# Rope attention and two MLPs on one core: when the next pair's q and k are prepared beside the attention units

## The chip, the cores and the metric

The kernel runs on one core of a Trainium2 chip. The core has five instruction streams that matter here: TensorE (PE; PEld are its weight loads), VectorE (DVE), ScalarE (ACT), GpSimd (POOL) and SyncE (SP), which issues the DMAs. The metric is the device time of one execution in microseconds (us), lower is better; of several executions the median is taken.

## The reference, cut to what matters

Attention over 4 batches and 8 heads of 576 tokens and 64 dimensions, and behind it two MLPs over the 2304 tokens (512 to 2048 to 512), each with an activation of its own.

```python
def rotate(x):
    x1, x2 = (x[..., :half], x[..., half:])
    return np.concatenate([x1 * cos - x2 * sin, x1 * sin + x2 * cos], axis=-1)
q_rot, k_rot = (rotate(q), rotate(k))
scores = scale * np.matmul(q_rot, k_rot.transpose(0, 1, 3, 2))
scores = scores - np.max(scores, axis=-1, keepdims=True)
attn = np.exp(scores)
attn = attn / (np.sum(attn, axis=-1, keepdims=True) + 1e-09)
return np.matmul(attn, v).astype(np.float32)
...
h = x @ w_in
g = np.where(pos, h, np.where(neg, 0.0, (h + beta) ** 2 / (4.0 * beta)))
return (g @ w_out).astype(np.float32)
```

The second MLP is the same with `s * relu(h) ** 2 + b` in between.

## The kernel before

Precision comes from parts: an fp32 operand is split into a high part (rounded to the format that TensorE reads at full rate) and a low part (the rest), and products are summed over the parts.

**Attention.** Two heads of a batch make a pair; there are 16 pairs (0 to 15), and each has nine units (`UNITS`): four blocks of 128 query rows for either head, and a fifth in the middle (unit 4 of the pair) that holds the 64 remaining rows of both heads. The units of all pairs are counted through, 0 to 143; unit 36 is the first of pair 4. A unit goes through all engines: TensorE makes its scores (`sc`, L357, in one of two PSUM buffers), VectorE takes the row maxima (`nm`, L359), ScalarE the exponentials (`p`, L364), TensorE transposes `p` (`tp`, L379), and VectorE or ScalarE copies that out of PSUM (`pt`, L386 for the second head, L384 for the first, L382 for the unit in the middle). After each half of a pair the products with v follow (`av`, `rm`), and a result `u`.

**Preparing a pair.** Each pair's q and k must be rotated and split before its first score:

- q: GpSimd multiplies it by the table (four instructions, `qin<-qin,tab_sb`), VectorE adds the two halves (L294, "the sum"), ScalarE writes the high part (L308, once for each head) and VectorE the low part (L309, once for each head), into one of two tiles `qs0`, `qs1`, which the pairs use in turn.
- k: GpSimd multiplies (four instructions, `kin<-kin,tab_sb`) and adds (two), ScalarE casts the high part (L321, "the cast"), GpSimd subtracts (two more, `fp32r` in the rows), and SP copies the parts on to `kh` (four DMAs, L326) and `kz` (two, L329), of which there are two tiles each as well.

**Beside it.** ScalarE, VectorE and GpSimd also convert the MLP's weights, half a slice at a time (`convert()`: L134 first on ScalarE, L135 to L138 on VectorE, L139 on ScalarE, two steps on GpSimd), and from pair 6 on TensorE works through the first MLP's products (L181, `h` and `y`) between the units. After the attention the rest of the MLPs follows, with an order on TensorE that is written out by hand.

**What sets the order.** Before that, a scheduler puts the instructions of each engine in an order when the program is built, from the order in which the code names them and what each needs; on the chip each engine then works through its own list in order. `with tc.issue_after(x):` asks that what is recorded inside, as far as it runs on x's engine, stands behind x in that list. It makes no wait on the chip by itself. `maxs[n]` and `exps[n]` are the maxima and the exponentials of unit n, `parts[1]` the cast and the subtraction of pair 1's k. `do_load(n)`, called once for each unit, names the preparations. Before, it named q's whole preparation of pair i+1 at unit 0 of pair i, and k's at unit 2, tied to nothing (but pair 2's q); so the scheduler places each step as early as its inputs and its buffers let it.

Of the kernel before, what the change touches and what calls it, by code (L numbers as in the profile page):

```python
# [14 lines left out]
ALU = mybir.AluOpType  # L15
# [51 lines left out]
def kernel(ctx, tc, qq, kk, vv, tab, ww1, ww2, s, b, out):  # L67
    nc = tc.nc
# [516 lines left out]
    def do_load(n):  # L585
        if n == 0:
            with tc.issue_after(turned):
                turned_by(tq, QP[1])
                lay_q(0, tq, QP[1], None)
        elif n in (1, 2):  # L590
            with tc.issue_after(maxs[n]):
                if n == 1:
                    turned_by(tq, QP[2])
                else:
                    lay_q(0, tq, QP[2], None)
        if n < len(units):
            i, k = units[n]
            if i + 1 < NPAIR:
                if i == 0 and k in (2, 6):
                    with tc.issue_after(maxs[k]):  # L600
                        turned_by(qk_in["q", 1], HALVES[k // 6])
                if i == 0 and k in (4, 5, 7, 8):
                    with tc.issue_after(maxs[k]), tc.issue_after(exps[k - 1]):
                        lay_q(1, qk_in["q", 1], HALVES[k // 6], None, [int(k in (5, 8))])
                if i and k == 0:
                    with ExitStack() if i > 1 else tc.issue_after(parts[1][1]), ExitStack() if i > 1 else tc.issue_after(maxs[9]):
                        rope_pair(i + 1, "q", nc.gpsimd, nc.vector, None)
                elif k == 2:
                    with ExitStack() if i else tc.issue_after(exps[2]), ExitStack() if i else tc.issue_after(lowest):
                        rope_pair(i + 1, "k", nc.gpsimd, nc.gpsimd, [nc.gpsimd, nc.vector])  # L610
                elif k == 7:
                    load_v(i + 1)
                elif k in (4, 6) and i + 2 < NPAIR:
                    load_qk(i + 2, "q" if k == 4 else "k")

        if n in range(33, 51, 2) or n in range(70, 110, 4):
            with tc.issue_after(exps[n - 14]):
                convert()

        if n in PARK_AT and parking:  # L620
            with tc.issue_after(exps[n - 4]):
                parking.pop(0).park(wst, scratch)()
# [581 lines left out]
```

## Time and profile before

| | |
|---|---|
| median of 3 runs | 1116.61 us (1113.03 to 1118.2) |
| profiled execution | 1117.65 us, of which the profile's span is 1115.9 us |
| busy share of the span | PE 96%, PEld 88%, DVE 69%, ACT 57%, POOL 38% |
| units of attention | 144, exponentials from 15.3 to 417.9 us |
| granted TensorE clock | 0.998 on the mean |

The span runs from the first to the last instruction. A busy time is the time that an engine's instructions cover; TensorE's ends are modelled, so small gaps between its instructions do not show. In the rows, "x14" is a count, and a row of the timeline that ends in [0.70 <-DVE pt L386] says that the engine was idle for 0.70 us before this instruction and that line 386 on VectorE ended it.

### The profile page before, as it was taken

The page shows a single profiled execution, that of the slowest core. Times are in us where ns is not written, and L with a number is a line of the kernel's source. Part 1 is how long each engine was busy: PE and PEld are TensorE (multiplying, and loading weights), DVE is VectorE, ACT ScalarE, POOL GpSimd, SP SyncE. Part 2 cuts the span into 40 slices and gives each one's busy share as a digit, 9 for nine tenths or more (in the row PEclk, how much of TensorE's full clock was granted, in tenths as well). Part 3 has the DMA queues.
Part 4 walks back from the last instruction along what each step waited for, and adds up shares of the span by engine and source line. Part 5 has one row for each costly group of instructions (what it writes and reads, how often), then busy time and mean ns, then how long its engine had stood idle before and what let it go on. Part 6 is the DMA issues. An engine that isn't in the chain of part 4 may idle for free.

```text
span 1115.9 us, 20052 instructions
## 1 busy us (share of the span) xinstructions
PE 1074.3 (96%) x7296; PEld 981.3 (88%) x7296; DVE 775.0 (69%) x1445; ACT 631.0 (57%) x1440; POOL 426.9 (38%) x564
## 2 busy tenths in 40 slices
PE   5899999989999999999999999999999999999998
PEld 3666788878888889999999999999999999999997
DVE  7888987768576663454757667866777778677754
ACT  5777776766666665454545455474554448334431
POOL 6998977686473332332544445110212110000000
PEclk9999999999999999999999999999999999999999
DMA  8665856656675544655465673231322853221221
GB/s 240 168 191 167 253 160 208 207 165 188 202 227 166 174 151 138 220 171 190 149 183 203 211 238 116 86 112 59 113 89 90 301 171 116 82 83 42 80 63 36
DMA packets 109762, 173.24 MB, mean 155 GB/s; under 512 B 29408, under 2 KB 80608, under 8 KB 109664
## 3 DMA queue, kind: packets, MB, share of 16 engines
q1 hardware_dynamic: 109664, 171.97, 49.1%
q8 instruction: 57, 0.93, 0.4%
q14 instruction: 41, 0.34, 0.1%
HBM read 110.10 MB, written 48.56 MB: 142 GB/s over the span
## 4 chain that ended last, share of the span: by engine, by line
PE 81%; DVE 5%; DMA 5%; POOL 3%; ACT 3%; issue 2%; SPq 0%; POOLq 0%; ACTq 0%
PE hps L181 15%; PE sum L940 14%; PE yps L856 6%; PE yps L855 6%; PE yps L854 6%; PE y L181 5%; PE sc L357 5%; PE yps L790 4%; PE yps L791 4%; PE yps L792 4%; PE av L405 4%; PE h L181 4%; PE tp L379 3%; DMA wraw<-in_ww 1%; DMA kz<-kin 1%
## 5 line engine op out<-in xcount | busy, mean ns | idle before, releaser
L181 PE MATMUL hps<-xh,w 128*128 128x288 f32 (+4 forms) x640 | 163.4, 324 | 0.0
L357 PE MATMUL sc<-kh,qs 128*128 128x288 f32 x336 | 102.7, 328 | 24.5 <-ACT p L364 13.5
L359 DVE TENSOR_REDUCE nm<-sc 128x1 f32<-128x576 f32 x144 | 106.5, 748 | 24.9 <-PE sc L357 24.4
L364 ACT ACTIVATE p<-sc,nm 128x576 f32<-128x576 f32 x144 | 106.7, 742 | 28.6 <-DVE nm L359 26.2
L948 ACT ACTIVATE four<-four,b_sb,s_sb 128x480 f32<-128x480 f32 x64 | 47.4, 782 | 127.2 <-DVE four L947 127.2
L856 PE MATMUL yps<-gh,w 128*128 128x480 f32 (+1 forms) x320 | 118.5, 370 | 0.0
L854 PE MATMUL yps<-gh,w 128*128 128x480 f32 (+1 forms) x320 | 118.4, 370 | 0.0
L855 PE MATMUL yps<-gl,w 128*128 128x480 f32 (+1 forms) x320 | 118.4, 370 | 0.0
L96 POOL TENSOR_TENSOR wm<-wm,w 128x256 f32<-128x256 f32 x80 | 69.5, 888 | 119.1 <-ACT w L139 62.5
L181 PEld LDWEIGHTS hps<-xh,w 128*128 128x128 f32 x640 | 113.2, 188 | 1.0
L357 PEld LDWEIGHTS sc<-kh,qs 128*128 128x128 f32 x336 | 63.5, 192 | 45.7 <-ACT p L364 27.0
L181 PE MATMUL hps<-xl,w 128*128 128x288 f32 (+4 forms) x320 | 103.7, 324 | 0.0
L790 PE MATMUL yps<-gh,w 128*128 128x288 f32 (+3 forms) x288 | 93.2, 324 | 1.4 <-DVE yp L797 0.7
L357 PE MATMUL sc<-kz,qs 128*128 128x288 f32 x336 | 93.8, 301 | 0.0
L791 PE MATMUL yps<-gl,w 128*128 128x288 f32 (+3 forms) x288 | 92.8, 322 | 0.0
L792 PE MATMUL yps<-gh,w 128*128 128x288 f32 (+3 forms) x288 | 92.8, 322 | 0.0
L379 PE MATMUL tp<-ident,p 128*128 128x128 f32 x576 | 87.2, 276 | 4.0 <-DVE pt L386 3.4
L96 POOL TENSOR_TENSOR wm<-wm,raw 128x256 f32<-128x256 f32 x16 | 12.6, 806 | 176.8 <-ACT raw L139 176.8
L181 PE MATMUL y<-gh,w 128*128 128x288 f32 x320 | 75.0, 305 | 2.0 <-DVE ptr L397 0.9
L379 PEld LDWEIGHTS tp<-ident,p 128*128 128x128 f32 x576 | 70.5, 142 | 6.2 <-DVE pt L386 4.1
L405 PE MATMUL av<-pt,vin 128*64 128x256 f32 (+1 forms) x512 | 75.7, 417 | 0.0
L107 DVE TENSOR_TENSOR gl<-hps,gh 128x288 fp32r<-128x288 f32 (+4 forms) x88 | 46.4, 527 | 40.4 <-ACT gh L103 40.2
(154 smaller groups left out, 2905.9 us busy)
## 6 DMA issues: line engine op xcount, KB each, us to landing
wraw<-in_ww SPq DMA_DIRECT2D x56, 512.0 KB, 4.4
w<-parkd SPq DMA_DIRECT2D x24, 512.0 KB, 6.1
kin<-in_k SPq DMA_DIRECT2D x15, 576.0 KB, 4.4
qin<-in_q SPq DMA_DIRECT2D x15, 576.0 KB, 4.8
kh<-kin SPq DMA_DIRECT2D x60, 144.0 KB, 2.9
parkd<-wraw SPq DMA_DIRECT2D x16, 512.0 KB, 3.2
xs<-y1d SPq DMA_DIRECT2D x32, 240.0 KB, 2.7
xd<-u SPq DMA_DIRECT2D x16, 288.0 KB, 2.7
```

The lines of the kernel that those rows point to most:

```text
L181: m = nc.tensor.matmul(out_ps, l, r, start=(i == 0), stop=(i == n - 1))
L357: nc.tensor.matmul(sc[:, half, o:o + n], l, r[:, k0:k0 + n], start=m == 0, stop=m == len(todo) - 1)
L364: exps[i * 9 + k] = nc.scalar.activation(p, sc[:, :, :288], AF.Exp, bias=nm, scale=1.0, accum_out=sums_t[i][:, col:col + 1]).ins
L379: m = nc.tensor.transpose(v[:, c, :], p[:, c * P:(c + 1) * P], ident)
L405: nc.tensor.matmul(ps[j * D:(j + 1) * D, :n], v[:, kt, j, :], pt[g][:, kt, j, :], start=kt == 0, stop=False)
L790: nc.tensor.matmul(acc, wh, gh, start=f == 0, stop=False)
L791: nc.tensor.matmul(acc, wh, gl, start=False, stop=False)
L792: nc.tensor.matmul(acc, wl, gh, start=False, stop=last)
L854: nc.tensor.matmul(acc, wh, gh, start=f == 0, stop=False)
L855: nc.tensor.matmul(acc, wh, gl, start=False, stop=False)
L856: nc.tensor.matmul(acc, wl, gh, start=False, stop=last)
L940: nc.tensor.matmul(acc, l, r, start=j == 0, stop=j == len(t) - 1)
```

## The change

The preparation of pair i+1 is taken apart for i of 1 and more (pairs 2 to 15) and named at different units of pair i: q's product at unit 0; q's sum at unit 4, behind the maxima of unit 3; the two heads' parts at units 5 and 6, behind the maxima of the unit before and the exponentials of the one before that; k's product and sum at unit 2, as before; k's cast, subtraction and copies at unit 3, the cast behind the exponentials of unit 2. Apart from that, `convert()` at units 70 to 106 has its first step on ScalarE behind the exponentials of ten units back, where it was fourteen. No instruction is added or removed; instructions stand elsewhere in the engines' lists.

```diff
                 if i == 0 and k in (4, 5, 7, 8):
                     with tc.issue_after(maxs[k]), tc.issue_after(exps[k - 1]):
                         lay_q(1, qk_in["q", 1], HALVES[k // 6], None, [int(k in (5, 8))])
+                if i:
+                    t = qk_in["q", i + 1]
+                    if k == 0:
+                        with ExitStack() if i > 1 else tc.issue_after(parts[1][1]):
+                            pool_tt(out=t, in0=t, in1=tab_sb, op=ALU.mult)
+                    elif k == 4:
+                        with tc.issue_after(maxs[n - 1]):
+                            nc.vector.tensor_tensor(out=t[:, 1], in0=t[:, 0], in1=t[:, 1], op=ALU.add)
+                    elif k in (5, 6):
+                        with tc.issue_after(maxs[n - 1]), tc.issue_after(exps[n - 2]):
+                            lay_q(i + 1, t, WHOLE[0], None, [k - 5])
                 if i and k == 0:
-                    with ExitStack() if i > 1 else tc.issue_after(parts[1][1]), ExitStack() if i > 1 else tc.issue_after(maxs[9]):
-                        rope_pair(i + 1, "q", nc.gpsimd, nc.vector, None)
+                    pass
                 elif k == 2:
                     with ExitStack() if i else tc.issue_after(exps[2]), ExitStack() if i else tc.issue_after(lowest):
-                        rope_pair(i + 1, "k", nc.gpsimd, nc.gpsimd, [nc.gpsimd, nc.vector])
+                        if i == 0:
+                            rope_pair(i + 1, "k", nc.gpsimd, nc.gpsimd, [nc.gpsimd, nc.vector])
+                        else:
+                            t = qk_in["k", i + 1]
+                            pool_tt(out=t, in0=t, in1=tab_sb, op=ALU.mult)
+                            pool_tt(out=t[:, 1], in0=t[:, 0], in1=t[:, 1], op=ALU.add)
+                elif k == 3 and i:
+                    with tc.issue_after(exps[n - 1]):
+                        lay_k(i + 1, qk_in["k", i + 1], WHOLE[0], None)
                 elif k == 7:
                     load_v(i + 1)
...
         if n in range(33, 51, 2) or n in range(70, 110, 4):
-            with tc.issue_after(exps[n - 14]):
+            with tc.issue_after(exps[n - (10 if n > 60 else 14)]):
                 convert()
```

What it does to the lists is shown at three places. VectorE before, at units 39 to 41 (in pair 4): the maxima (L359) of units 39 and 40, and behind them the sum for `qin_1595`, the q of pair 7.

```order
L359 TENSOR_REDUCE nm_1225<-sc_1220 128x1
L386 COPY pt_1209<-tp_1243 128x4x128
L359 TENSOR_REDUCE nm_1264<-sc_1253 128x1
L294 TENSOR_TENSOR qin_1595<-qin_1595 128x576
L359 TENSOR_REDUCE nm_1284<-sc_1279 128x1
L386 COPY pt_1209<-tp_1302 128x4x128
L420 RECIPROCAL sume_1340<-sume_1340 128x5
```

VectorE after, at units 39 to 41; the sum (now L612) is that of `qin_966`, the q of pair 5, and its two low parts follow.

```order
L359 TENSOR_REDUCE nm_1210<-sc_1205 128x1
L612 TENSOR_TENSOR qin_966<-qin_966 128x576
L386 COPY pt_1194<-tp_1238 128x4x128
L359 TENSOR_REDUCE nm_1259<-sc_1248 128x1
L309 SCALAR_TENSOR_TENSOR qs1_108<-qin_966,qs1_108 64x576
L359 TENSOR_REDUCE nm_1280<-sc_1275 128x1
L386 COPY pt_1194<-tp_1300 128x4x128
L309 SCALAR_TENSOR_TENSOR qs1_108<-qin_966,qs1_108 64x576
L420 RECIPROCAL sume_1340<-sume_1340 128x5
```

The sum stood three pairs ahead of its use and stands one pair ahead now; sum and parts are in one place, each between the maxima of two units, and in ten of the fourteen pairs the sum stands directly in front of a copy of `pt` (in four before).

ScalarE before, at units 19 and 20 (in pair 2), with the cast of `kin_775`, the k of pair 4.

```order
L134 ACTIVATE wa_1019<-wraw_1017 128x512
L438 COPY r_656<-rm_651 128x384
L321 CAST kin_775<-kin_775 128x576
L384 COPY pt_686<-tp_688 128x4x128
L364 ACTIVATE p_668,sums_595<-sc_661,nm_666 128x576
```

ScalarE after, from the exponentials of unit 29 to those of unit 31 (in pair 3): the same cast, and the high parts of `qin_727`, the q of pair 4.

```order
L364 ACTIVATE p_902,sums_834<-sc_895,nm_900 128x576
L321 CAST kin_775<-kin_775 128x576
L364 ACTIVATE p_902,sums_834<-sc_921,nm_926 128x576
L308 ACTIVATE qs0_107<-qin_727 64x576
L384 COPY pt_910<-tp_968 128x4x128
L364 ACTIVATE p_962,sums_834<-sc_949,nm_960 128x576
L308 ACTIVATE qs0_107<-qin_727 64x576
```

The cast moved ten units back here, and 3 to 18 units over the pairs; the high parts moved by 3 to 7 units.

GpSimd before, around the subtraction of pair 4's k (the last row with `kin_775`): its two sums, the factors `eb` of a result, and the product of pair 5's q stand ahead of it.

```order
L96 TENSOR_TENSOR kin_775<-kin_775 128x288
L96 TENSOR_TENSOR kin_536<-kin_536 128x288 x2
L96 TENSOR_TENSOR kin_775<-kin_775 128x288
L422 COPY eb_643<-sume_640 128x256
L96 TENSOR_TENSOR qin_970<-qin_970,tab_sb_106 128x2x144 x4
L96 TENSOR_TENSOR kin_775<-kin_775 128x288 x2
```

GpSimd after, around the same subtraction: the products of pair 5's q and k and the steps of a conversion (`wm`, `w`) stand ahead of it.

```order
L96 TENSOR_TENSOR qin_966<-qin_966,tab_sb_106 128x2x144 x4
L96 TENSOR_TENSOR wm_1084<-wm_1084,w_1080 128x256 x2
L96 TENSOR_TENSOR kin_1014<-kin_1014,tab_sb_106 128x2x144 x4
L422 COPY eb_877<-sume_874 128x256
L96 TENSOR_TENSOR w_1080<-wm_1084,wa_1083 128x256 x2
L96 TENSOR_TENSOR kin_775<-kin_775 128x288 x2
L96 TENSOR_TENSOR kin_1014<-kin_1014 128x288 x2
```

The subtraction moved back behind work for pair 5. The first steps of the seven conversions in the second batch (L134 on ScalarE) stood behind the exponentials of units 68, 72, 78, 80, 84, 88 and 91, and stand behind those of 69, 73, 77, 80, 83, 85 and 90 now. Behind the attention all lists are the same.

## Rows read from the trace of the kernel before

**Rows 1.** The page, part 1: busy time, share of the span, instructions.
```profile
PE 1074.3 (96%) x7296; PEld 981.3 (88%) x7296; DVE 775.0 (69%) x1445; ACT 631.0 (57%) x1440; POOL 426.9 (38%) x564
```
**Rows 2.** Busy time by stretch: us, PE, PEld, DVE, ACT, POOL (instructions), clock, DMA share, GB/s.
```profile
33.00:134.00 101.00, 93.07 (x678) 66.61 (x677) 87.44 (x142) 77.33 (x183) 90.65 (x118) 1.00 0.68 197
134.00:300.00 166.00, 153.15 (x1160) 132.83 (x1159) 124.57 (x223) 114.72 (x285) 119.00 (x160) 0.99 0.61 186
300.00:418.00 118.00, 116.67 (x913) 104.30 (x913) 79.86 (x150) 80.58 (x201) 47.70 (x70) 1.00 0.61 185
```
**Rows 3.** TensorE's waits from 33 to 418 us: total, times, longest.
```profile
PE sc L357 <- ACT p L364: 10.4, 13, 1.9
PE tp L379 <- DVE pt L386: 3.4, 3, 1.7
```
**Rows 4.** VectorE's waits from 33 to 418 us.
```profile
DVE qin L294 <- POOL qin L96: 12.3, 7, 3.5
...
DVE qs L309 <- ACT qs L308: 3.5, 6, 0.8
```
**Rows 5.** ScalarE's waits from 33 to 418 us.
```profile
ACT kin L321 <- POOL kin L96: 3.3, 4, 1.2
...
ACT qs L308 <- PE sc L357: 2.4, 5, 1.0
```
**Rows 6.** Timeline from 33.8 to 42 us: start, length, engine, line, tiles, idle time before.
```profile
33.86 1.33 DVE L294 TENSOR_TENSOR qin<-qin 128x576 f32<-128x576 f32 x1
...
36.57 0.66 PE L379 MATMUL tp<-ident,p 128*128 128x128 f32 x4 [1.03 <-DVE pt L386]
...
40.54 0.74 ACT L364 ACTIVATE p<-sc,nm 128x576 f32<-128x576 f32 x1 [1.82 <-DVE nm L359]
...
41.42 0.40 PE L357 MATMUL sc<-kh,qs 128*128 128x288 f32 x1 [1.69 <-ACT p L364]
```
**Rows 7.** Timeline from 101.3 to 105 us.
```profile
101.51 1.27 DVE L294 TENSOR_TENSOR qin<-qin 128x576 f32<-128x576 f32 x1 [1.88 <-POOL qin L96]
...
104.09 0.44 PE L392 MATMUL tr<-ident,p 128*128 128x128 f32 x2 [0.70 <-DVE pt L386]
```
**Rows 8.** Timeline of TensorE at six of its stalls.
```profile
51.59 0.40 PE L357 MATMUL sc<-kh,qs 128*128 128x288 f32 x1 [0.27 <-ACT p L364]
...
72.81 0.40 PE L357 MATMUL sc<-kh,qs 128*128 128x288 f32 x1 [1.23 <-ACT p L364]
...
109.86 0.40 PE L357 MATMUL sc<-kh,qs 128*128 128x288 f32 x1 [1.19 <-ACT p L364]
...
125.93 0.40 PE L357 MATMUL sc<-kh,qs 128*128 128x288 f32 x1 [0.62 <-ACT p L364]
...
195.78 0.66 PE L379 MATMUL tp<-ident,p 128*128 128x128 f32 x4 [0.69 <-DVE pt L386]
...
362.90 0.40 PE L181 MATMUL y<-gh,w 128*128 128x288 f32 x1 [0.21 <-ACT pt L382]
```
**Rows 9.** The sum's line: count, shortest, median and longest (ns), first and last start.
```profile
L294 DVE TENSOR_TENSOR qin<-qin x14: 879/1266/1345, 33.9 to 315.6; 128x576 f32<-128x576 f32 x14
```
**Rows 10.** Timeline: k's cast and subtraction, unit 29's exponentials, pair 4's first score.
```profile
57.02 0.68 ACT L321 CAST kin<-kin 128x576 fp32r<-128x576 f32 x1
...
62.45 2.51 POOL L96 TENSOR_TENSOR kin<-kin 128x288 fp32r<-128x288 f32 x2
...
75.01 1.75 POOL L96 TENSOR_TENSOR kin<-kin 128x288 fp32r<-128x288 f32 x2 [0.78 <-ACT kin L321]
...
78.00 0.74 ACT L364 ACTIVATE p<-sc,nm 128x576 f32<-128x576 f32 x1 [0.43 <-DVE nm L359]
...
89.04 0.40 PE L357 MATMUL sc<-kh,qs 128*128 128x288 f32 x1
```
**Rows 11.** The copies on to `kz` (L329): from issue to landing.
```profile
DMA to landing us min/median/max: 2.4/3.6/5.2
```
**Rows 12.** Busy time from 152 to 157 us, columns as in rows 2.
```profile
152.00:157.00 5.00, 4.26 (x21) 4.25 (x22) 3.40 (x7) 4.64 (x12) 5.00 (x7) 0.66 0.45 134
```

## Prediction, before the result was known

> **What bounds the kernel now.** I read the page first: TensorE is busy for 1074.3 of 1115.9 us [rows 1]. The change removes none of its work, so what can be won or lost is its idle time of 41.6 us, and of that only what lies where the lists differ, from unit 9 to the last (33 to 418 us). The stretches [rows 2] say how much that is: 7.9 us in 33 to 134 (attention alone), 12.9 in 134 to 300 and 1.3 in 300 to 418 (with the MLP in between), 22.1 in all. In the first stretch VectorE and GpSimd are busy for 87 and 90% as well: there a step that stands badly in a list has little slack behind which to hide. After 300 us the MLP's products cover nearly everything.
>
> Who ends TensorE's idle time? Mostly the exponentials, whose end frees a buffer of scores (10.4 us, 13 times), then VectorE's copies of `pt` (3.4) [rows 3]. Both lists also hold the preparation of coming pairs, and these steps wait at the head of their engine's list: the sum for GpSimd's product 12.3 us in seven waits, the low part for the high part 3.5 [rows 4], k's cast for GpSimd 3.3, the high part for scores that still read its tile 2.4 [rows 5]. What stands behind a waiting step, the next maxima or exponentials, waits too.
>
> I then went through all of TensorE's stalls in 33 to 418 us in the timeline and looked at what the two engines had done in the 4 us before.
>
> - Behind a *wait* of a preparing step: 12 stalls, from 72.81 (1.23 us) to 362.90 (0.21) [rows 8], 8.4 us together. The plainest is at 101.51: the sum for pair 7, not needed for two more pairs, waits 1.88 us and takes 1.27; maxima and copy come behind it, and TensorE stands for 0.70 [rows 7].
> - Behind the *length* of preparing steps that waited for nothing: 6 stalls, from 36.57 (1.03) [rows 6] to 195.78 (0.69) [rows 8], 5.5 us. At 38.6 two low parts and a sum follow each other, the exponentials start 1.82 us late and TensorE stands for 1.69 [rows 6].
> - Others (conversions, the MLP's steps, and stalls where I saw no preparing step at the head): the remaining 8.2 us.
>
> **The change part by part.** *The sum* goes from right behind GpSimd's product to one pair ahead of its use. The product is then done for many units, so the seven waits should go. *The high and low parts* go from the end of the pair that still reads the tile to the middle of the next, where the tile is free: their waits for scores go. *The cast* goes one to two pairs back, behind sums that are long done: its waits go. So the 8.4 us of the first group are taken off whole.
>
> The lengths stay: 14 sums, 28 high and 28 low parts, 14 casts, in the same number and size, on engines that feed TensorE. What changes is that each now stands alone between two units. So I take off the 5.5 us of the second group and charge each pair anew for lone steps. Lone sums that waited for nothing were five before; behind two of them TensorE stood, 0.62 us at 125.93 and 0.69 at 195.78 [rows 8], which is 0.26 for each of five. Fourteen cost 3.7 us. The bounds are 0 (three of five cost nothing) and 0.69 each, 9.7 us, since the sum now mostly stands in front of a copy of `pt`, as it did at 195.78. For parts and cast the nearest row is the single high part ahead of the exponentials at 51.59, a stall of 0.27 [rows 8]; one such a pair is 3.8 us. The bounds are 0 and 1.19 a pair, 16.7 us: that is 109.86, where two high parts and a conversion's step stood ahead of the exponentials [rows 8].
>
> *The copies of k* move back with the cast, four and two DMAs a pair, and on SP four loads of v now stand between the two kinds. Are they late? For pair 4 the cast now follows unit 29's exponentials, which start at 78.00 and end, with the read of their sums, some 0.9 us later; the first score of pair 4 was at 89.04 [rows 10]. Cast 0.68, subtraction 1.75 (free) to 2.51 us, landing 3.6 after the issue [rows 10, 11]. GpSimd took the subtraction up at once at 75.01 in one case and 4.75 us after the cast's end in another (57.70 to 62.45) [rows 10]; I take the middle, 2.4. That gives 78.9 + 0.7 + 2.4 + 1.75 + 3.6 = 87.4, 1.7 us to spare; with the longer wait and subtraction 90.4, 1.4 late. From 134 us on a pair takes longer and the spare grows, so five pairs at most (2 to 6) are in question. I charge nothing, with bounds of 0 and 5 x 1.4 = 7.0 us.
>
> *The conversions' tie* moves seven first steps by three units at most, and no stall of TensorE's in these waits is ended by a converted weight. I charge nothing; the cover is the lead with which weights are converted, and if it were gone the MLP's first products would wait by name for L96 or L139.
>
> The sum: -8.4 - 5.5 + 3.7 + 3.8 = **-6.4 us**. The profiled execution took 1117.65 us (1.75 around its span), 1.04 above the median of the three runs. On that execution the forecast is 1111.25, on the median **1110.2**, 0.6% faster. With half of the new costs it is 1106.4, with one and a half of them 1114.0: the likeliest case's own range.
>
> One stretch speaks for a larger gain. Behind two of TensorE's stalls the granted clock left 2.4 GHz for 1.2 GHz for a while: from 152 to 157 us its mean is 0.66 of the full rate [rows 12], so 5 x 0.34 = 1.7 us were lost. I leave that in the sum; if the dip goes with the stalls, the sum is -8.1 and the time 1108.5, and of the forecast's chance below I give this 0.10. The Trainium skill, *TensorE: Matmul & The Clock Gate*, Part 1, says that half rate is the array's default state and that activity releases it, by which fewer stalls would take the dip along. The row agrees in that the rate fell behind stalls; that it would not have fallen without them no run here shows.
>
> **The rivals.**
>
> 1. *The lone steps cost next to nothing*, and all 13.9 us go, the dip's 1.7 as well: 1116.6 - 15.6 = 1101.0. For it: three of five lone sums cost nothing, and in the middle of a pair TensorE has the longer unit. Against it: VectorE is 87% busy in the first stretch [rows 2].
> 2. *The stalls only move.* Work and engines are the same, and if each pair pays 1.0 us for its lone steps (14 in all) the time is 1116.6, no change. For it: the sum in front of the copy, as at 36.57, cost 1.03 [rows 6].
> 3. *The sum meets GpSimd's steps in the middle.* Before, it started as GpSimd's product ended, and took 0.88 to 1.35 us, 1.27 on the median [rows 9]. Beside a step of GpSimd's that has just begun it could take its own 0.88 and the rest of that step, up to 0.88 more (half of 1.75 [rows 10]): 1.76, and 14 x 0.49 = 6.9 us more than in the sum, 1117.1. The Trainium skill, *SBUF — State Buffer*, section on the two separate sides, gives the ground: a VectorE operation with two SBUF inputs and a GpSimd operation that reads SBUF lock one pair of ports, each for its whole length. The trace agrees so far as no sum is shorter than 0.88, and shows none above 1.35.
> 4. *k comes late: slower.* One mechanism: GpSimd, 90% busy in the first stretch [rows 2], has pair 5's k product (four steps of about 0.88), two steps of a conversion and `eb` ahead of pair 4's subtraction, some 5 us if they start only at the cast's end. With 5.1 of wait, a subtraction of 2.51 and a landing of 5.2 [rows 11] pair 4's `kz` lands at 92.4, 3.4 late; five such pairs cost 16.8 us and give 1127.0. It decides against the change from 6.4 / 5 = 1.3 us a pair. Against it: GpSimd has the same work as before, and need not wait with it for the cast.
> 5. *The lone steps cost their upper bounds* (9.7 + 16.7): -13.9 + 26.4 = +12.5, 1129.1. Every pair would have to be like the worst row.
>
> **How the numbers follow.** The three runs spread over 0.5%, so a difference under 0.5% (1111.0 to 1122.2 counts as no change) can't be told. Chances: the forecast 0.52, of which 0.33 lie below 1111.0 and 0.19 above; rival 1 0.14; rival 2 0.15; rival 3 0.04; rival 4 0.10; rival 5 0.05. So faster 0.47, same 0.38, slower 0.15. The range reaches from rival 1 to above rivals 2 and 3 and leaves 4 and 5 out: 1101.0 to 1120.0.
>
> **What would show it.** Right: in the waits from 33 to 418 us the sum's wait for GpSimd, the high part's for scores and the cast's for GpSimd are gone; TensorE's idle time there falls from 22.1 to about 16 us, and the exponentials' share of it falls most; no score waits for a DMA. Wrong: stalls of `tp` or `tr` behind `pt` L386 once a pair near its unit 4 (rivals 2 and 5); sums above 1.35 us (rival 3); scores at a pair's start that wait for a DMA of `kz` or `kh`, with GpSimd's subtraction over 4 us behind the cast (rival 4). The forecast is wrong too if the time after 418 us changes, since its lists do not.

## The result and the profile after

The changed kernel took 1120.39 us (median of 20 runs, 1116.61 to 1128.5), the kernel before 1115.83 (20 runs, 1111.22 to 1118.5) on the same chip: a ratio of 1.0055, 95% interval 1.0043 to 1.0067 (from all the runs; the two medians alone give 1.0041). It is slower, where 0.6% faster was forecast; 1120.39 lies 0.4 us above the range. The profiled execution of the changed kernel took 1118.57 us, 1.8 below its own median, with a mean granted clock of 1.000.

The page's line of busy time, which answers to [rows 1], and the busy time by stretch, which answers to [rows 2] (us of the stretch, then busy time of TensorE, its weight loads, VectorE, ScalarE and GpSimd, then the clock, the DMA share and GB/s):

```profile
PE 1074.5 (96%) x7296; PEld 980.0 (88%) x7296; DVE 770.2 (69%) x1445; ACT 630.0 (56%) x1440; POOL 424.9 (38%) x564
```

```profile
33.00:134.00 101.00, 93.76 (x675) 66.47 (x675) 84.08 (x141) 76.40 (x179) 79.88 (x106) 1.00 0.62 182
134.00:300.00 166.00, 154.93 (x1191) 134.95 (x1190) 127.49 (x231) 118.93 (x295) 117.53 (x159) 1.00 0.66 191
300.00:418.00 118.00, 112.47 (x875) 99.23 (x874) 74.24 (x139) 75.89 (x191) 58.24 (x85) 1.00 0.62 192
```

TensorE's idle time from 33 to 418 us is 7.2 + 11.1 + 5.5 = 23.8 us, where 22.1 were before and some 16 were forecast. It fell by 2.5 us ahead of 300 us and rose by 4.2 behind. Over the whole span it is 42.3 us (1116.8 less 1074.5) where it was 41.6, so this one execution holds little of the 6 us that the runs lost; its own time, 1118.57, is only 0.9 us above the one profiled before. GpSimd's work slid to the right: 10.8 us less of it lies in the first stretch, 10.5 more in the third.

The waits from 33 to 418 us (engine and line, what it waited for, total, times, longest), TensorE's, VectorE's and ScalarE's, against [rows 3 to 5]:

```profile
PE sc L357 <- ACT p L364: 6.0, 11, 1.0
PE rm L433 <- POOL eb L422: 2.3, 2, 1.8
PE tr L392 <- ACT ys L507: 2.0, 2, 1.5
PE y L181 <- ACT ys L507: 1.4, 1, 1.4
PE y L181 <- ACT pt L382: 1.4, 2, 1.2
PE sc L357 <- DMA kz<-kin: 1.3, 1, 1.3
```

```profile
DVE wm L135 <- ACT wa L134: 26.9, 16, 4.8
DVE nm L359 <- PE sc L357: 26.5, 34, 2.7
DVE u L441 <- ACT r L438: 18.2, 9, 3.2
DVE sume L420 <- ACT sume L419: 10.8, 6, 3.4
```

```profile
ACT p L364 <- DVE nm L359: 24.6, 36, 2.5
ACT wa L134 <- POOL w L96: 12.3, 10, 3.4
ACT ys L507 <- POOL yq L96: 7.8, 2, 5.7
```

The waits that the change was about are gone from these rows: the sum's for GpSimd's product, the high part's for scores, the cast's for GpSimd. TensorE waits 6.0 us for exponentials and not 10.4. But VectorE's wait for the first step of a conversion (`wm` for `wa`) went from 10.8 us to 26.9, and new rows have come: `rm` for GpSimd's `eb`, `kz` from a DMA, products and transposes behind `ys`, which waits for GpSimd's `yq`. One of them in the timeline:

```profile
79.01 4.09 POOL L96 TENSOR_TENSOR kin<-kin,tab_sb 128x288 f32<-128x288 f32 x4
81.08 1.37 DVE L309 SCALAR_TENSOR_TENSOR qs<-qin,qs 64x576 fp32r<-64x576 f32 x1
82.48 0.19 DVE L420 RECIPROCAL sume<-sume 128x5 f32<-128x5 f32 x1
83.05 0.39 POOL L422 COPY eb<-sume 128x256 f32<-128x256 f32 x1
83.50 0.44 PE L433 MATMUL rm<-ident,eb 128*128 128x128 f32 x2 [1.78 <-POOL eb L422]
```

k's product holds GpSimd for 4.09 us, and the reciprocal comes behind a low part of 1.37; `eb` follows at 83.05, and TensorE stands for 1.78. In another profile of the same kernel (*the change, again*, below) this stall does not appear: single waits come and go from one execution to the next.

### The profile page after: what moved, and what is told of

It is laid out like the page before. It is cut to its first block, busy times and chain, and to the rows that moved or that the text cites. A ratio compares the mean times of both kernels' runs of the same rounds, so it can differ in the third digit from the quotient of the medians.

```text
span 1116.8 us, 20030 instructions
## 1 busy us (share of the span) xinstructions
PE 1074.5 (96%) x7296; PEld 980.0 (88%) x7296; DVE 770.2 (69%) x1445; ACT 630.0 (56%) x1440; POOL 424.9 (38%) x564
## 4 chain that ended last, share of the span: by engine, by line
PE 77%; POOL 8%; DVE 6%; DMA 3%; ACT 3%; issue 2%; SPq 0%; POOLq 0%; DVEq 0%; ACTq 0%
PE hps L181 15%; PE sum L958 14%; PE yps L874 6%; PE yps L873 6%; PE yps L872 6%; PE sc L357 4%; PE y L181 4%; PE yps L808 4%; PE yps L809 4%; PE yps L810 4%; PE h L181 4%; POOL kin L96 4%; PE av L405 3%; PE tp L379 3%; DVE nm L359 2%
## 5 line engine op out<-in xcount | busy, mean ns | idle before, releaser
L359 DVE TENSOR_REDUCE nm<-sc 128x1 f32<-128x576 f32 x144 | 107.1, 749 | 28.7 <-PE sc L357 27.8
L107 DVE TENSOR_TENSOR gl<-hps,gh 128x288 fp32r<-128x288 f32 (+4 forms) x88 | 46.4, 527 | 41.2 <-ACT gh L103 41.1
```

The source lines that it names most:

```text
L359: maxs[i * 9 + k] = nc.vector.tensor_reduce(out=nm, in_=sc[:, :, :288], axis=AX.XY, op=ALU.max, negate=True).ins
```

## The experiments

Each kernel was timed against the kernel before in five rounds on one chip (4 to 12 runs of it, 16 to 29 of before). How many instructions stand elsewhere than before is counted as those that have to be taken out of an engine's list until the rest is in before's order. By that count the ties, which name 14 sums, 56 parts and 14 casts with k's subtractions and copies, move 197 instructions on VectorE, 167 on ScalarE, 163 on GpSimd, 114 on SP and 288 matmuls. The edit of the conversions' bound (14 to 10) moves none: with it and without it all five lists are the same.

| kernel | elsewhere on PE, VectorE, ScalarE, GpSimd, SP | ratio to before, interval | mean clock, and of before beside it |
|---|---|---|---|
| the change, again | 288, 197, 167, 163, 114 | 1.0056 (1.0034 to 1.0077) | 0.9959, 0.9976 |
| q's tie alone | 260, 190, 159, 147, 67 | 1.0046 (1.0031 to 1.0061) | 0.9928, 0.9976 |
| k's tie alone | 252, 159, 130, 143, 115 | 1.0058 (1.0039 to 1.0077) | 0.9929, 0.9976 |
| steps alone, five lists set | 0, 42, 42, 138, 84 | 1.0245 (1.0224 to 1.0266) | 0.9872, 0.9975 |
| rest alone, five lists set | 288, 165, 135, 52, 42 | 1.0418 (1.0392 to 1.0444) | 0.9813, 0.9975 |
| steps alone, three lists set | 0, 42, 42, 154, 118 | 1.0268 (1.0251 to 1.0284) | 0.9878, 0.9974 |
| rest alone, three lists set | 288, 165, 135, 67, 61 | 1.0213 (1.0190 to 1.0236) | 0.9932, 0.9974 |
| fill bound 3 | 129, 86, 80, 55, 26 | 1.0053 (1.0034 to 1.0072) | 0.9960, 0.9975 |
| fill bound 3 and the ties | 268, 195, 172, 167, 115 | 1.0034 (1.0014 to 1.0055) | 0.9944, 0.9974 |
| fill budget 0.60 | 575, 141, 157, 45, 31 | 1.0030 (1.0012 to 1.0048) | 0.9972, 0.9975 |
| fill budget 0.60 and the ties | 579, 201, 207, 167, 115 | 1.0046 (1.0027 to 1.0066) | 0.9948, 0.9974 |
| late budget 0.90 | 468, 85, 103, 18, 31 | 1.0061 (1.0040 to 1.0081) | 0.9947, 0.9974 |
| late budget 0.90 and the ties | 588, 209, 199, 160, 116 | 1.0065 (1.0040 to 1.0090) | 0.9968, 0.9974 |
| before, GpSimd and SP free | 0, 0, 0, 30, 29 | 1.0051 (1.0037 to 1.0065) | 0.9955, 0.9974 |
| before, ten delays | 0, 0, 0, 0, 0 | 1.0046 (1.0030 to 1.0062) | 0.9965, 0.9974 |
| before, 18 local moves | 0, 11, 7, 0, 0 | 1.0035 (1.0020 to 1.0050) | 0.9968, 0.9979 |
| conversions one unit later | 0, 9, 6, 11, 2 | 1.0023 (1.0007 to 1.0040) | 0.9971, 0.9979 |
| before itself | none | 0.9995 (0.9975 to 1.0014) | 0.9984, 0.9975 |

**Each tie by itself.** The first theories were that k's cast and copies come late and crowd GpSimd (K), that q's sum and parts, now close together, stand in front of copies and maxima (Q), or that more dips of the granted clock make the time (C). In the first kernel k's part is as before, in the second q's, in the third nothing is undone:

```diff
-                        if i == 0:
-                            rope_pair(i + 1, "k", nc.gpsimd, nc.gpsimd, [nc.gpsimd, nc.vector])
-                        else:
...
-                elif k == 3 and i:
-                    with tc.issue_after(exps[n - 1]):
-                        lay_k(i + 1, qk_in["k", i + 1], WHOLE[0], None)
+                        rope_pair(i + 1, "k", nc.gpsimd, nc.gpsimd, [nc.gpsimd, nc.vector])
```

> Only q's sum and parts are tied to units of the pair in front; k's preparation and the conversions are as before. Theory K (the loss comes from k's cast: GpSimd's subtraction now waits for a late cast, its later work slips, and factors, k copies and accumulations come late): this kernel has none of it, ratio to before 0.995 to 1.001. Theory Q (sum and both low parts in one place make VectorE late once a pair): the whole loss is here, ratio 1.004 to 1.008. Theory C (TensorE's clock falls to 1.2 GHz more often, and that is the loss): the time of single runs goes with their mean granted clock, about 1 us for each 0.001, and at a clock of 0.998 to 1.000 this kernel is within 2 us of before.

> Only k's cast, subtraction and copies are tied to the pair in front; q and the conversions are as before. Theory K: ratio 1.004 to 1.010, GpSimd busy under 84 us in the stretch from 33 to 134 us (79.9 in the changed kernel, 90.7 before). Theory Q: 0.997 to 1.001. Theory C: as slow as its mean clock says, whichever of the two it is.

> The changed kernel once more beside the other two on one chip: ratio 1.004 to 1.007 as measured. Theory C: its runs have a lower mean clock than those of the kernel before (0.996 against 0.998 or more), and the runs of both kernels with a clock of 0.998 or more differ by under 2 us. Theories K and Q: they differ by 4 us or more at the same clock.

The change again is 1.0056. Either tie alone costs as much as both, 1.0046 and 1.0058. Each of K and Q comes true in its own kernel and fails in the other, and if both held the two losses should add up: neither explains it. For C there is something. What the clock takes is at most its loss times the span (all of it if TensorE works through the whole of it): the mean clocks of the two are lower by 0.0048 and 0.0047 than before's, so at most 5.4 and 5.2 of their 5.1 and 6.5 us. For the change it is 0.0017, at most 1.9 of 6.2 us. So the clock can have a part, from a third to all of it. Single runs at the same clock say more. Of the change, 3 of 12 runs had a mean clock of 0.998 or more, and took 1116.4 us on the mean; 21 of before's 29 runs beside it had that, and took 1113.9. The 2.5 us between them lie between the answers put down for theory C (under 2) and for K and Q (4 or more): a part of the loss goes with the clock, and a part is there without it. With q's tie alone no run reached 0.998, so for that kernel the two can't be told apart in this way.

**The places and the rest, exchanged.** Since the ties move far more than they name, I wrote the lists out by hand. `in_order` ties each instruction to the one ahead of it in a row of numbers, and the scheduler has nothing left to choose:

```diff
+def in_order(tc, nc):
+    at = {i.name: i for i in nc.cur_bb.bb.instructions}
+    for row in ROWS:
...
+                if last is not None:
+                    tc.add_manual_dep(i, last.name, edge, reason="order")
+                last = i
```

> Each engine's list is written out whole. Everything stands in the order of the kernel before, TensorE's list unchanged, except the steps that make q and k ready (sum, high and low parts, cast, subtraction, GpSimd's products, the loads and copies of q and k): these stand at the units at which the changed kernel has them (42 instructions moved on VectorE, 42 on ScalarE, 138 on GpSimd, 84 on SP). Theory M (the new places of these steps cost the time: they collide with other steps there): about as slow as the change, ratio 1.004 to 1.007 of before. Theory R (the ties make the scheduler lay the rest anew, 288 matmuls, 155 other instructions on VectorE, some 125 on ScalarE among it, and that costs): ratio 0.994 to 1.001, the -6.4 us of the prediction or part of it. Theory T (lists and places are only good together): slower than before, 1.003 or more, here and in the opposite kernel.

> The opposite kernel: every list in the order of the changed kernel, but the steps that make q and k ready stand at the units at which the kernel before has them. Theory M: ratio 0.998 to 1.002 of before, and its waits of sum, parts and cast back in the profile. Theory R: ratio 1.004 to 1.010. Theory T: 1.003 or more. Under each theory the old waits (sum for GpSimd's product, high part for scores, cast for GpSimd) come back.

Both are far slower, 1.0245 and 1.0418, which only theory T had foreseen, and not by so much. In these kernels line numbers are 21 higher. TensorE's waits from 33 to 450 us, of the steps alone and of the rest alone:

```profile
PE sc L378 <- DMA kz<-kin: 6.8, 3, 3.3
PE sc L378 <- ACT p L385: 6.3, 10, 1.2
```

```profile
PE sc L378 <- ACT p L385: 31.1, 22, 9.9
```

With the steps alone `kz` comes late, with the rest alone the exponentials. I had set GpSimd and SP by a mere count of what stands ahead, so the next two leave these two lists to the scheduler, and a third does the same to before's own lists. The diff to the kernels above is that `ROWS` has three rows and not five.

> As the kernel with the steps alone, but only TensorE's, VectorE's and ScalarE's lists are written out (the kernel before, with q's sum and parts and k's cast at the units of the changed kernel); GpSimd's and SP's lists are left to the scheduler, which fits them to these. In the kernel with the steps alone, where I had set those two by rank, TensorE's stalls were 38.4 us against 25.4, 6.8 of them waits for copies of k. Theory S (that setting cost it, the steps' places cost nothing): ratio 0.995 to 1.002, no score that waits over 1 us for a copy of k. Theory T (places and lists are only good together): 1.008 or more. If the ties cost the time by the new laying of the rest alone: under 1.003.

> The opposite: the changed kernel's lists on TensorE, VectorE and ScalarE, with q's sum and parts and k's cast at the units of the kernel before; GpSimd and SP left to the scheduler. Theory S: 1.003 to 1.008, as the change, since the rest is the changed kernel's. Theory T: 1.01 or more, the waits of a conversion's first step for GpSimd (31.4 us where I had set GpSimd by rank) still there.

> The control for both: the kernel before's own lists on TensorE, VectorE and ScalarE, nothing moved in them; GpSimd and SP left to the scheduler without the ties of before, which puts 30 and 29 instructions elsewhere. If 30 instructions on a queue of copies and loads and on GpSimd are enough to cost time: 1.002 to 1.005. If not: 0.999 to 1.001.

1.0268 and 1.0213: setting GpSimd and SP by count was not what cost it with the steps alone; with the rest alone it was about half (1.0418 before), and the wait of the conversions' first step for GpSimd fell from 31.4 us to 11.3, against theory T's sign. Theory S falls by both ratios. Places and lists go together (a sum or a cast half a pair later holds its tile longer, and with it the loads that wait for the tile; that is argued), so neither half of the change can be judged by moving it into the other kernel's lists.

The third one was meant to be even and is 1.0051. A part of it I can name: without the ties of the first pair a subtraction on GpSimd for `kz` comes late, TensorE's first stalls are the two below, and the exponentials of unit 9 start at 36.0 us, where before's two profiles have 33.9 and 33.6. The rest I cannot.

```profile
15.02 0.61 PE L378 MATMUL sc<-kz,qs 128*128 128x288 f32 x1 [2.60 <-POOL kz L117]
16.64 0.61 PE L378 MATMUL sc<-kz,qs 128*128 128x288 f32 x1 [0.77 <-POOL kz L117]
```

**Controls that name no step of q or k.** The MLP's steps beside the attention are bound to other exponentials, or get another budget:

```diff
-        with tc.issue_after(exps[min(n, len(units)) - 4]):
+        with tc.issue_after(exps[min(n, len(units)) - 3]):
```

```diff
-            run_fill(0.62 if n < 76 else 0.92)
+            run_fill(0.60 if n < 76 else 0.92)
```

> A control that names no step of q or k: the kernel before, with the MLP's steps in the attention bound to the exponentials three units back instead of four. The scheduler lays 129 matmuls, 86 instructions on VectorE and 80 on ScalarE anew. If any new laying of these tuned lists costs time (the wide form of theory R): ratio 1.002 to 1.007. If only that of the change does: 0.998 to 1.002.

> A second control: the kernel before with a budget of 0.60 instead of 0.62 for the MLP's steps beside a unit. The scheduler lays 575 matmuls, 141 instructions on VectorE and 157 on ScalarE anew, about as many as the ties do on VectorE and ScalarE. The wide form of theory R: ratio 1.002 to 1.007. The narrow form: 0.998 to 1.002. In both controls theory C (the granted clock dips more often in other layings) shows as a mean clock under that of the runs of before beside it by 0.002 to 0.005.

1.0053 and 1.0030. Layings that have nothing to do with the change are slower too, one of them as much. Where the budget's kernel loses can partly be seen in its profile, behind the attention:

```profile
481.65 0.37 PE L790 MATMUL yps<-gh,w 128*128 128x288 f32 x1 [1.73 <-ACT gh L103]
450.00:500.00 50.00, 47.73 (x346) 47.25 (x345) 22.90 (x45) 23.43 (x59) 17.56 (x20) 0.97 0.56 184
```

All four kernels with another budget, here and below, have this stall in their profiles, of 1.7 to 2.4 us, and the clock at 0.97 in this stretch; in all other profiles but those of the four kernels that cross the two kernels' lists it is at most 0.9 us, with the clock at full rate. From the start of the last exponentials to the end these four take 701.6 to 704.0 us and the others 695.3 to 698.8. The new budget also puts 25 (0.60) or 47 (0.90) of TensorE's matmuls behind the last scores elsewhere, where the ties change no order. So 3 to 9 us of these four executions belong to the work behind the attention.

That layings which name no step of q or k are slower as well raised the question whether a kernel measured in this way comes out slower whatever it is, so before was measured against itself:

> The kernel before, unchanged, measured against itself as the others were. All eight kernels measured against it so far, two controls that move 30 to 60 instructions on two queues or add 19 us of idle copies on ScalarE among them, came out 3 to 7 us slower or more. Theory W (the lists of before are a picked set, nearly every other laying is slower): ratio 0.999 to 1.001, single runs 1111 to 1119, and a second profile of it whose stalls before 450 us are under the 25.4 us of the first, since the first profiled execution (1117.65) lies 2 to 3 us above the medians of before. Theory V (a kernel measured against before comes out slower whatever it is): ratio 1.003 to 1.006.

0.9995: theory V falls. Its second profile has an idle TensorE for 21.3 us from 33 to 418 us, so the profile that I predicted from was not a bad one in that.

**Three layings, each with the ties and without.** This tells the ties from the laying. The diffs are those of the controls (0.90 for 0.92 in the third), on the kernel before and on the changed one.

> The changed kernel with a budget of 0.60 instead of 0.62 for the MLP's steps beside a unit, against the control that has the same budget without the ties (1.0030). Theory W (before's lists are a picked laying; the ties as such cost nothing or little): no slower than that control by more than 0.002, so 0.997 to 1.005. Theory Q (the ties cost 5 to 6 us wherever they stand): 1.0030 + 0.0055, that is 1.0065 or more.

> The changed kernel with the MLP's steps bound to the exponentials three units back, against the control with this bound and without the ties (1.0053). Theory W: 0.999 to 1.007. Theory Q: 1.009 or more.

> The changed kernel with 0.90 instead of 0.92 as the later budget of the MLP's steps. Its partner, the kernel before with the same budget, runs beside it. Theory W: within 0.002 of the partner, either way. Theory Q: above the partner by 0.0045 or more.

> The kernel before with 0.90 instead of 0.92 as the later budget: 468 matmuls, 85 instructions on VectorE and 103 on ScalarE laid anew, 18 on GpSimd. Theory W: 1.002 to 1.006, as the other controls. If only layings that move GpSimd's steps cost time: within 0.001 of before.

The ties make 1.0046 of 1.0030, 1.0034 of 1.0053 and 1.0065 of 1.0061: differences of +0.0016, -0.0019 and +0.0004, with half-widths near 0.003 each (those of the two intervals added in squares; the partners of the first two pairs ran on two chips, each against before on its own). Theory Q of these four, that the ties cost 0.0055 wherever they stand, is excluded by each pair; so is the forecast gain of 6.4 us, 0.0057. The ties as such are worth nothing that can be told, one way or the other, on these three layings. By that, what the change lost on before's laying is that laying, and not the places of the steps it names; this is an inference from the pairs: the rest alone, which was to show it directly, came out far slower.

**A price for a stall.** Before's five lists, with ten copies of one column put ahead of the exponentials of each of ten units:

```diff
+    idle = const.tile([P, 1], F32, name="idle")
+    for _ in range(100):
+        nc.scalar.copy(idle, eps)
```

> The price of a stall, by itself: the kernel before's lists on all five engines, none moved, with ten copies of one column each (about 0.2 us apiece, some 2 us together) put ahead of the exponentials of ten units, 20 to 101 in steps of nine. From the profile: how much TensorE's stalls grow. Theory A (a stall is paid twice, by itself and by the clock that falls behind it): the mean clock falls by 0.002 or more and the time grows by 1.5 to 2.5 times the added stalls. Theory B (stalls are paid once, and the other layings are slower for something else): the clock stays within 0.001 and the time grows by 0.8 to 1.2 times the added stalls. If every delay stalls TensorE in full, that is 10 x 2 = 20 us of stalls.

```profile
L1175 ACT COPY idle<-eps x100: 185/191/215, 58.2 to 287.4; 128x1 f32<-128x1 f32 x100
```

That is 100 x 0.191 = 19.1 us of ScalarE's time in front of exponentials, and the kernel is 5.1 us slower. TensorE's idle time from 33 to 418 us is 21.1 us in its profile, no more than before, and the mean clock is lower by 0.0009, at most 1.0 us. Neither theory fits: the added stalls cannot be read from one execution, and a price per stall stays open. What it shows is that at least some 14 of these 19 us ahead of the exponentials are absorbed.

**Only the waiting steps, one or two rows down.** This is what the ties meant to do, without a new laying. Writing the lists out adds nothing by itself: with before's own lists in `ROWS` the program is that of before, instruction for instruction, with its waits. Of before's lists, one piece on VectorE as an example, where the sum for pair 7 waits in [rows 7]:

```diff
-L294 TENSOR_TENSOR qin_1595
 L359 TENSOR_REDUCE nm_1284
 L386 COPY pt_1209
+L294 TENSOR_TENSOR qin_1595
```

> What the ties meant to do, without laying anything else anew: the lists of the kernel before written out on all five engines, and in them only 18 steps moved, each one or two rows down: seven sums, four low parts, four casts of k and three high parts that waited at the head of their list in its profile (14.1 and 2.8 us, 3.3 and 1.9 us of the waits). What then stands ahead is a maximum, a copy or an exponential that was ready. If the prediction's first term is right (8.4 us of TensorE's stalls stand behind such waits and go with them): ratio 0.993 to 0.997. If the stalls only move (the ties were worth nothing on three other layings): 0.999 to 1.002. If any difference from these lists costs time, 18 rows too: 1.003 or more.

> A small control: the kernel before with the conversions one unit later, in both stretches. TensorE's list is unchanged; 9 instructions stand elsewhere on VectorE, 6 on ScalarE, 11 on GpSimd and 2 on SP, none of them a step of q's or k's preparation that the ties name. If so small a difference costs time: 1.002 to 1.005, as with 30 instructions on GpSimd and 29 on SP (1.0051). If not: 0.999 to 1.001.

(The sums' waits are 12.3 us, as [rows 4] have them; the 14.1 in the expectation is a slip.) 1.0035: not even this gains. VectorE's wait for scores before, then VectorE's and TensorE's waits from 33 to 418 us with the 18 local moves, and the busy time by stretch:

```profile
DVE nm L359 <- PE sc L357: 24.4, 33, 1.7
```

```profile
DVE nm L380 <- PE sc L378: 35.6, 37, 2.5
...
DVE qin L315 <- POOL qin L117: 3.4, 1, 3.4
...
DVE qs L330 <- ACT qs L329: 0.7, 2, 0.4
```

```profile
PE sc L378 <- ACT p L385: 8.6, 10, 1.7
PE h L202 <- ACT pt L405: 2.3, 1, 2.3
PE y L202 <- DVE gl L128: 2.1, 2, 1.6
PE tp L400 <- DVE pt L407: 1.8, 3, 0.9
```

```profile
33.00:134.00 101.00, 94.49 (x681) 67.81 (x680) 86.91 (x141) 77.57 (x183) 90.64 (x119) 0.98 0.69 198
134.00:300.00 166.00, 154.68 (x1160) 135.16 (x1159) 124.95 (x223) 115.43 (x285) 119.31 (x160) 0.97 0.61 186
300.00:418.00 118.00, 117.05 (x911) 103.99 (x910) 79.99 (x149) 80.01 (x199) 48.19 (x70) 1.00 0.61 185
```

The sums wait 3.4 us once and not 12.3 in seven, the low parts 0.7 and not 3.5. VectorE then waits for scores instead, 35.6 us where it was 24.4: it came free earlier and had nothing to do. TensorE waits less for exponentials and for `pt` (8.6 and 1.8 us, where [rows 3] have 10.4 and 3.4), and more for ScalarE's `pt` and for `gl` (2.3 and 2.1, where they were 1.3 and 1.2). It is idle for 18.8 us in this execution, 3.3 less than in [rows 2], but the clock of the first two stretches is 0.98 and 0.97, and the time, 1117.71, is within 0.1 us of the execution before that [rows 1] show. So in this execution a part of the stalls did go, and the time came back in the clock: its mean is 0.994 against 0.998, at most 0.004 x 1116 = 4.5 us. Over all runs the clock is lower by only 0.0011, at most 1.2 of the 3.9 us, and the five runs with a clock of 0.998 or more took 1116.7 us on the mean where before's fifteen took 1112.6. So most of this loss is not the clock, and where it lies is open.

The small control, 28 instructions in all, is 1.0023 with 0.0007 as its lower bound: between the two answers that I had put down.

## Why the prediction was wrong

*What bounds the kernel* held in part. TensorE's idle time was read right, and its work is the same. But its idle time is not all that can be won or lost: with q's tie alone it is busy for 1077.8 us and idle for 41.1, less than before's 41.6, in an execution 3.0 us longer.

```profile
PE 1077.8 (96%) x7296; PEld 986.1 (88%) x7296; DVE 771.3 (69%) x1445; ACT 629.0 (56%) x1440; POOL 430.6 (38%) x564
```

The same matmuls took longer there, at a mean clock of 0.992. The sum has a dip that may be won (0.10), and no term for a clock that is lost.

*The waits go.* Right, for the sum, the high part and the cast, and no wait of that kind is left above the last row shown. So was "no score waits for a DMA" but for one: `kz` of pair 6, 1.34 us.

*"So the 8.4 us of the first group are taken off whole."* This is the step that failed. It takes a stall that stands behind a wait to be made by it. The 18 local moves took these waits away (but for one of 3.4 us) and left all else in place; TensorE's idle time fell by 3.3 us in the profiled execution, not 8.4, and the kernel was 3.9 us slower. When VectorE doesn't wait for GpSimd, it waits for scores, and other rows end TensorE's idle time. The second group, the 5.5 us behind lengths, is taken off by the same reasoning; no run tests it by itself.

*The charges for lone steps* can't be told from the rest. Lone sums became shorter on the median, not longer:

```profile
L612 DVE TENSOR_TENSOR qin<-qin x14: 748/913/1441, 37.9 to 380.7; 128x576 f32<-128x576 f32 x14
```

0.91 us on the median where [rows 9] have 1.27, and 0.75 at the least, so the 0.88 that rival 3 takes for a sum's own length is too long. The ties' own balance is the pairs' +0.0016, -0.0019 and +0.0004. Rival 2, *the stalls only move*, comes nearest to that: its sum of zero fits the pairs. Its 1.0 us a pair for lone steps is seen nowhere.

*The step that was not there.* I took the lists around the named steps for given, while the ties lay 288 matmuls anew, and on VectorE and ScalarE 197 and 167 instructions, where they name 42 each. I had both programs' lists, and showed three places where the named steps had moved, and did not count the others. Every laying measured that is not before's own was slower, by 0.23 to 0.65% where no lists were crossed, and before against itself was even. That is the term of some +5 us that the forecast and the rivals lack. That the lists of before are the fastest of many that were tried would explain it; it is argued from these twelve, and not shown. Not all of the twelve tell of the attention alone: the four with another budget lose part behind it, and the one with GpSimd and SP free part ahead of unit 9.

*The time after 418 us* did change: the last exponentials start at 421.0 us and not 417.9, and what follows takes 695.8 us and not 698.0. The boundary had moved: the last exponentials start later against TensorE's other work (4437 of its matmuls start behind them and not 4452), so this sign of a wrong forecast was badly chosen.

*k late* (rival 4) happened once in the change's profile, for 1.34 us. The sign of *the sum meets GpSimd* (rival 3), sums above 1.35 us, came twice there, 1.38 and 1.44 us; one of 5.77 came with k's tie alone, where q's sum is not tied. They are not what the 5 us are made of. *The conversions' tie*: it moves no instruction, not seven as I had it.

*The clock dip left in the sum.* The changed kernel's profiled execution has none, so its profile speaks for the gain that I gave 0.10, but over the runs the mean clock is lower, by 0.0017, and it is lower in every other laying. Its share of the loss goes from 0.3 of 3.3 us (budget 0.60) to 5.4 of 5.1 (q's tie alone), as upper bounds.

What stays open is why before's lists are better at the same clock, but for the four with another budget, where a part is seen behind the attention. Single profiles don't tell: TensorE's idle time from 33 to 418 us is 18.6 to 24.5 us in all that did not cross lists, and 18.8 us go with 1.0035 as 21.3 go with 0.9995. A profile of every execution would be needed. No version here beats before.

## What to carry to other kernels

Before a tie is priced, count what it moves in the lists that it does not name. In this kernel each of twelve other layings came out 0.2 to 0.65% behind, and an edit has to win more than that to show. A wait that was taken off an engine which itself waits for the bottleneck became another wait of that engine: price a stall by what would end it next, not by the row that ends it now. And measure an edit of such a kernel against the same edit on a second and a third laying, and before against itself; the ratio of 1.0055 on one laying did not come back as a cost of the ties on three others.

## What the runs showed of the hardware

One sum took 5.77 us, with k's tie alone, four and a half times its median in [rows 9], and TensorE stood behind it for 5.78. VectorE's and GpSimd's rows of the timeline there:

```profile
123.70 5.77 DVE L294 TENSOR_TENSOR qin<-qin 128x576 f32<-128x576 f32 x1 [0.44 <-POOL qin L96]
129.39 0.74 DVE L359 TENSOR_REDUCE nm<-sc 128x1 f32<-128x576 f32 x1
```

```profile
123.61 0.82 POOL L96 TENSOR_TENSOR kin<-kin 128x288 f32<-128x288 f32 x1
124.36 0.83 POOL L96 TENSOR_TENSOR xl<-xs,xh 128x288 fp32r<-128x288 f32 x1
125.13 0.81 POOL L96 TENSOR_TENSOR kin<-kin 128x288 f32<-128x288 f32 x1
125.88 0.74 POOL L96 TENSOR_TENSOR w<-wm,wa 128x256 fp32r<-128x256 f32 x1
126.56 1.56 POOL L96 TENSOR_TENSOR kin<-kin 128x288 fp32r<-128x288 f32 x2
128.03 0.14 POOL L275 MEMSET vin<- 64x64 f32 x1
128.14 0.71 POOL L96 TENSOR_TENSOR w<-wm,wa 128x256 fp32r<-128x256 f32 x1
128.91 0.15 POOL L275 MEMSET vin<- 64x64 f32 x1
```

GpSimd's steps follow each other without a gap from 123.61 to 129.06, and the sum, begun at 123.70, ends only at 129.47, 0.41 us behind the last of them. The Trainium skill, *SBUF — State Buffer*, section on the two separate sides, has the two lock one pair of ports for whole instructions; the row agrees, and shows more than rival 3 allowed for, which was the rest of one step: this sum waited for all of them in a row. It is not the only one: with fill bound 3 and the ties one sum took 3.87 us, and with the rest alone and three lists set one took 3.13, each beside GpSimd's steps without a gap and ending 0.5 to 0.6 us behind the last. In 14 of the 20 profiles no sum of these fourteen is over 1.47 us; in the other six one is, from 1.79 to 5.77.

The clock behind that stall, in three stretches of 3 us (columns as in [rows 2]):

```profile
129.00:132.00 3.00, 0.94 (x4) 0.95 (x5) 2.97 (x6) 1.83 (x4) 0.45 (x2) 0.70 0.51 128
132.00:135.00 3.00, 3.00 (x14) 1.76 (x15) 2.49 (x5) 2.57 (x7) 0.00 (x0) 0.50 0.00 0
135.00:138.00 3.00, 3.00 (x21) 1.30 (x17) 1.55 (x3) 0.62 (x1) 0.00 (x0) 0.66 0.73 189
```

TensorE stood until 131.06, and when it worked again it had 1.2 GHz, through the whole second stretch, and came back to 2.4 GHz in the third. A stall of 1.78 us in the changed kernel's profile, at 83.50, brought no dip, and its clock is 1.00 in all stretches. Whether a stall is followed by a dip differs between executions of one kernel: single runs of the kernel before have mean clocks from 0.993 to 1.000, and its two profiles have one dip each, near 153 and near 235 us. The stall of 1.7 to 2.4 us behind the attention, in the four kernels with another budget, was followed by one each time.
